# Attention and two feed-forward layers on one core: the transposes and the order of the kernel's opening

## The chip, the core and the metric

The kernel runs on one core of a Trainium2 chip. The core has five engines with queues of their own: TensorE (PE; its weight loads are PEld), VectorE (DVE), ScalarE (ACT), GpSimd (POOL) and SyncE (SP), which here issues every transfer. An engine takes its instructions in the order of the program and waits, on semaphores, for what the others owe it. The metric is the device time of one execution in microseconds (us); lower is better.

## The reference

An attention over chunks of 32 positions (16 to the left, 8 to the right, 8 memory positions, so 64 keys a chunk), 4 batches of 8 heads, 768 positions, 64 a head; its output, 3072 tokens of 512, goes through a layer with a squared ReLU and then through a gated layer.

```python
scores = scale * np.matmul(q_c, k_full.transpose(0, 1, 3, 2))
scores = scores - np.max(scores, axis=-1, keepdims=True)
a = np.exp(scores)
a = a / (np.sum(a, axis=-1, keepdims=True) + 1e-09)
out[:, :, c_start:c_end] = np.matmul(a, v_full)
...
h = x @ w_in            # 512 -> 2048
r = np.maximum(h, 0.0)
x = (r * r) @ w_out     # 2048 -> 512
...
g = x @ w_gate          # 512 -> 1536
silu = g * (1.0 / (1.0 + np.exp(-g)))
return (silu * (x @ w_val)) @ w_out
```

## The kernel before

Attention is cut into 32 units of 96 positions (three chunks) with all eight heads. The tokens are cut into eight blocks of four units (384 tokens). For each block the first layer runs over 16 slices f of 128 hidden columns: 12 hidden matmuls (`hidden_pe`: high weight by high x, high weight by low x, low weight by high x, four of each) into one of two PSUM banks `hbank`, then ReLU and square on ScalarE, the low part of the square on VectorE, and 12 projecting matmuls (`project_pe`) into the banks `yb`. Numbers are kept as a high and a low part of type fp32r. The gated layer comes after all blocks.

The weights of the first layer arrive as raw 64-bit words, 1 MB a slice, and are turned into the two parts during the first block: a scaling on ScalarE (`scale1`, L329), a shift and a joining on VectorE (`shift1`, L333; `join1`, L342), the high part on ScalarE (`hi1`, L346) and the low part on VectorE (`lo1`, L350). The first block therefore has on top of its matmuls the conversion of all 16 slices, the attention of its own four units (0 to 3), and that of the next block's (4 to 7).

The opening is written out by hand: `OPENING` is a list of 328 tokens, a letter for a step and a number for the unit u or the slice f, and the queue of each engine holds its steps in the order of the list. After the list a planner takes over. The letters, with the lines of the profile:

- Q, V: load of queries and keys, of values (SP, L132, L137). S: 24 score matmuls (PE, L153), for units 0 to 3 into `yb0`, later into `abank`.
- M maximum, D subtraction, A sum, I reciprocal, N scaling (DVE, L165 to L229); E exponential (ACT, L177); F, G: exponentials of later units (ACT, L211), K their scaling (DVE).
- T: transposes of units 0 to 3 on PE (L191), C: the copies of the result to `pT` (ACT, L197, L198); U, W: block transposes of later units on VectorE (L238), four and three instructions.
- O: eight value matmuls (PE, L257). X, Y: high and low part of the unit's tokens (ACT L268, DVE L272).
- L: load of a weight slice (SP, L321); p, s, j, h, l: its five conversion steps as above.
- a, b: the first eight and the last four hidden matmuls (PE, L359); r, q, t: ReLU and the two squares (ACT, L367 to L378); g: the low part (DVE, L384); c, d: projecting matmuls (PE, L403).

The transposes of units 0 to 3 write 32x32 pieces into two tiles: `yb1`, which c0 needs next, and `hbank[0]`, which a0 needs next.

```python
turned = [yb1[:, 0:2, 0:NH * 32].rearrange("p c (h q) -> p c h q", q=32)]
turned.append(hbank[0][:, 0:NH * 32].rearrange("p (h q) -> p h q", q=32))
```

Of the kernel before, what the change touches and what calls it, by code (L numbers as in the profile page):

```python
# [11 lines left out]
ALU = mybir.AluOpType  # L12
# [6 lines left out]
GQ = 96  # L19
# [16 lines left out]
NI = NH // 2  # L36
# [10 lines left out]
OPENING = """
Q0 Q1 Q2 S0 Q3 M0 V0 D0 L0 S1 E0 A0 M1 Q4 I0 D1 L1 N0 S2 E1 s0 p0 T0 M2 A1 C0 V1 D2 O0 L2 I1 E2 S3 N1 X0 s1
T1 p1 A2 V2 Y0 C1 M3 L3 O1 I2 N2 p2 D3 T2 X1 j0 V3 E3 L4 C2 A3 I3 h0 Y1 N3 O2 p3 L5 j1 T3 X2 l0 h1 C3 Y2 V4
s2 S4 p4 L6 j2 O3 X3 s3 h2 Y3 p5 l1 Q5 a0 l2 L7 b0 p6 a1 j3 r0 b1 M4 q0 L8 t0 a2 s4 h3 g0 b2 j4 r1 q1 c0 L9  # L50
t1 l3 r2 d0 h4 g1 a3 s5 F4 l4 V5 b3 L10 c1 j5 G4 d1 s6 a4 j6 L11 h5 K4 b4 r3 q2 l5 t2 c2 h6 L12 g2 U4 q3 d2
t3 a5 r4 q4 g3 L13 t4 b5 W4 p7 c3 l6 r5 d3 q5 L14 s7 p8 O4 j7 S5 p9 a6 g4 h7 s8 Q6 j8 b6 t5 V6 c4 X4 l7 L15
r6 q6 d4 t6 g5 a7 h8 M5 s9 p10 b7 l8 c5 F5 Y4 d5 j9 a8 G5 g6 s10 b8 j10 c6 h9 K5 r7 d6 h10 U5 r8 q7 W5 t7
p11 l9 O5 q8 t8 S6 g7 V7 p12 l10 a9 Q7 X5 M6 b9 p14 s11 c7 F6 g8 s12 d7 Y5 a10 j11 G6 b10 s13 c8 j12 h11 d8
K6 r9 h12 a11 l11 q9 t9 U6 b11 r10 c9 q10 t10 g9 p13 l12 d9 r11 W6 q11 t11 p15 j13 O6 S7 g10 h13 s14 a12 Q8
X6 M7 b12 l13 F7 c10 j14 d10 G7 g11 a13 s15 Y6 b13 j15 h14 c11 r12 K7 h15 d11 l14 a14 q12 t12 U7 r13 b14 q13
c12 t13 g12 W7 d12 r14 q14 t14 l15 O7 S8 g13 g14 a15 X7 M8 b15 Y7 F8 c13 d13 r15 q15 t15 g15
"""


# [1 line left out]
def attention_moe_moe_kernel(ctx, tc, att, w1, w2, out):  # L62
# [9 lines left out]
    pe, act, dve, pool, sp = nc.tensor, nc.scalar, nc.vector, nc.gpsimd, nc.sync  # L72
# [10 lines left out]
    hbank = [ps.tile([128, 512], F32, name=f"hbank{i}") for i in range(2)]  # L83
    abank, yb0, yb1 = (ps.tile([128, 2, 512], F32, name=n) for n in ("abank", "yb0", "yb1"))
# [15 lines left out]
    def convert(raw):  # L100
# [262 lines left out]

# [263 lines left out]
    for c in range(NC2):  # L627
        a = QB * (P2 + c // 4) + (12, 26, 40, 52)[c % 4]
# [170 lines left out]
```

## Time and profile before

| | us |
|---|---|
| median of three runs | 1187.6 (1186.94 to 1189.79) |
| the profiled execution | 1183.89 |
| its span, first to last instruction | 1182.1 |
| TensorE busy in the span | 1151.9 (97%) |
| VectorE busy | 680.3 (58%) |
| ScalarE busy | 600.9 (51%) |
| GpSimd busy | 354.7 (30%) |

The profile is one execution with a record of every instruction. A busy share is an average over stages with different limits: the page's table of forty slices shows TensorE at 4 tenths in the first slice (the first 30 us), 8 in the second and 9 in all others but the last. So the time without TensorE lies at the start, and the views below are all of the first 110 us, beside the list of TensorE's waits up to the end.

### The profile page before, as it was taken

To read this page: it belongs to the slowest core of one execution; us is meant where nothing else is said; L and a number is where in the kernel's file an instruction comes from. 1 tells how busy PE (TensorE), PEld (TensorE's weight loads), DVE (VectorE), ACT (ScalarE), POOL (GpSimd) and SP (SyncE) were. 2 spreads that over 40 slices of the span, in tenths; PEclk is the share of its full clock that TensorE was granted. 3 is DMA by queue.
4 is the path that set the end of the run, shared out by engine and by line. 5 is a ranking of instruction groups with operands and counts; after the bars stand their busy time and mean duration, and the time that the engine had idled before them with its cause. 6 is when DMAs were issued, how large, how long until landed. Compare 5 with 4: busy or idle time off the path is not lost.

```text
span 1182.1 us, 21404 instructions
## 1 busy us (share of the span) xinstructions
PE 1151.9 (97%) x8448; PEld 1096.0 (93%) x8448; DVE 680.3 (58%) x1220; ACT 600.9 (51%) x1466; POOL 354.7 (30%) x301
## 2 busy tenths in 40 slices
PE   4899999999999999999999999999999999999998
PEld 4889999999999999999999999999999999999996
DVE  6798444646446465452515576656766576655554
ACT  4787445556555464555553354444445444453442
POOL 0000000202002021000043465646556465654541
PEclk9999999999999999999999999999999999999999
DMA  8921204536255262530223323353234433343221
GB/s 307 379 86 51 75 29 154 185 105 244 78 161 192 77 213 108 177 105 1 72 81 112 129 91 101 127 190 103 90 129 146 153 105 105 104 143 129 94 99 54
DMA packets 49445, 150.29 MB, mean 127 GB/s; under 512 B 4800, under 2 KB 14528, under 8 KB 44992
## 3 DMA queue, kind: packets, MB, share of 16 engines
q1 hardware_dynamic: 49344, 148.92, 36.4%
q8 instruction: 66, 1.08, 0.4%
q14 instruction: 35, 0.29, 0.1%
HBM read 122.16 MB, written 26.74 MB: 126 GB/s over the span
## 4 chain that ended last, share of the span: by engine, by line
PE 94%; DVE 4%; issue 1%; ACT 1%; DMA 0%; SPq 0%; DVEq 0%; ACTq 0%
PE hbank L527 30%; PE yb L403 21%; PE hbank L359 21%; PE yb L597 11%; PE abank L597 6%; PE abank L257 2%; PE abank L153 2%; DVE pT L238 1%; DVE w L350 1%; DVE cut L342 1%; PE yb L191 0%; DVE wraw L333 0%; DMA qk<-in_att_dram 0%; PE yb L153 0%; DVE gl L384 0%
## 5 line engine op out<-in xcount | busy, mean ns | idle before, releaser
L92 POOL TENSOR_TENSOR w<-gvraw,w 128x512 fp32r<-128x512 f32 x192 | 247.6, 1311 | 295.1 <-ACT w L89 295.1
L359 PE MATMUL hbank<-x,w 128*128 128x384 f32 x1536 | 289.3, 336 | 0.6 <-ACT x L268 0.6
L527 PE MATMUL hbank<-w 128*128 128x384 f32 x1440 | 281.8, 335 | 0.1
L359 PEld LDWEIGHTS hbank<-x,w 128*128 128x128 f32 x1536 | 269.8, 189 | 1.2 <-ACT x L268 0.9
L527 PEld LDWEIGHTS hbank<-w 128*128 128x128 f32 x1440 | 254.5, 188 | 9.2 <-DVE tmp L567 0.4
L403 PE MATMUL yb<-gh,w 128*128 128x384 f32 x1024 | 205.0, 337 | 0.0
L384 DVE TENSOR_TENSOR gl<-r,gh 128x384 fp32r<-128x384 f32 x128 | 74.5, 582 | 186.4 <-ACT r L378 185.8
L403 PEld LDWEIGHTS yb<-gh,w 128*128 128x128 f32 x1024 | 178.7, 188 | 2.2
L446 POOL TENSOR_TENSOR wraw<-cut 128x256 f32<-128x256 f32 x24 | 20.2, 862 | 454.5 <-DVE mx L203 337.0
L536 ACT CAST uh<-tmp 128x384 fp32r<-128x384 f32 x96 | 49.4, 514 | 184.7 <-DVE tmp L571 152.3
L367 ACT ACTIVATE r<-hbank 128x384 f32<-128x384 f32 x128 | 62.8, 491 | 153.9 <-PE hbank L359 152.0
L597 PE MATMUL yb<-w,uh 128*128 128x512 f32 x384 | 119.6, 392 | 0.0
L527 PE MATMUL hbank<-z,w 128*128 128x384 f32 x576 | 115.7, 335 | 0.0
L403 PE MATMUL yb<-gl,w 128*128 128x384 f32 x512 | 113.2, 334 | 0.0
L527 PEld LDWEIGHTS hbank<-z,w 128*128 128x128 f32 x576 | 102.1, 188 | 4.2
L89 ACT CAST w<-gvraw 128x512 fp32r<-128x512 f32 x192 | 99.3, 564 | 3.1 <-POOL w L92 2.1
L403 PEld LDWEIGHTS yb<-gl,w 128*128 128x128 f32 x512 | 90.9, 188 | 0.0
L211 ACT ACTIVATE prob<-abank,mx 96x72 f32<-96x72 f32 x224 | 68.2, 315 | 42.7 <-DVE mx L203 39.5
L238 DVE STREAM_TRANSPOSE pT<-prob 32x256 f32<-32x256 f32 x196 | 85.2, 435 | 3.2
L597 PEld LDWEIGHTS yb<-w,uh 128*128 128x128 f32 x384 | 70.5, 188 | 9.5 <-ACT o L603 0.4
L597 PE MATMUL abank<-w,uh 128*128 128x512 f32 x192 | 74.9, 397 | 0.0
L378 ACT ACTIVATE r<-r 128x384 f32<-128x384 f32 x128 | 67.3, 526 | 3.8
(94 smaller groups left out, 1285.2 us busy)
## 6 DMA issues: line engine op xcount, KB each, us to landing
wraw<-in_w_dram SPq DMA_DIRECT2D x34, 1024.0 KB, 7.8
gvraw<-w2g SPq DMA_DIRECT2D x48, 512.0 KB, 3.5
gvraw<-w2g SPq DMA_DIRECT2D x48, 384.0 KB, 3.1
qk<-in_att_dram SPq DMA_DIRECT2D x28, 464.0 KB, 4.0
spare<-w2o SPq DMA_DIRECT2D x24, 512.0 KB, 4.4
v<-in_att_dram SPq DMA_DIRECT2D x32, 256.0 KB, 3.3
y1d<-ys SPq DMA_DIRECT2D x8, 768.0 KB, 3.9
w2g<-wraw SPq DMA_DIRECT2D x12, 512.0 KB, 2.9
```

Of the source, the lines that this page charges most:

```text
L89: act.copy(hi, src)
L92: lo_engine.tensor_tensor(lo, src, hi.bitcast(F32), ALU.subtract)
L211: act.activation(probs[u % 2][:, h, 0:WK], s["s"][:, r, i], AF.Exp, bias=s["mx"][:, r, i:i + 1], scale=SCALE, accum_out=s["sm"][:, h],)
L238: dve.transpose(pT[row:row + 32, :, 32 * c:32 * c + 32], probs[u % 2][32 * c:32 * c + 32, :, col:col + 32],)
L359: pe.matmul(hbank[f % 2][:, 0:n], wt[:, k * 128:(k + 1) * 128], x[:, k, 0:n], start=i == 0, stop=i == 3 * KD - 1,)
L367: act.activation(r, hbank[f % 2][:, 0:n], AF.Relu)
L378: act.activation(r, r, AF.Square)
L384: dve.tensor_tensor(gl, g["r"], g["gh"].bitcast(F32), ALU.subtract)
L403: pe.matmul(ybank[e][:, 0:nt_of[t]], wt[:, c:c + 128], gtile[t, f][g], start=f == 0 and p == 0, stop=f == NF1 - 1 and p == 2,)
L527: pe.matmul(to, wt[:, k * 128:k * 128 + 128], z[:, k], start=n == 0, stop=n == 5)
L536: act.copy(uh, u)
L597: pe.matmul(outs[j], u[:, c:c + 128], wt, start=f == 0 and p == 0, stop=f == NF2 - 1 and p == 2)
```

## The change

Four edits. First, a unit's transposes on TensorE (T) are done a head at a time, eight matmuls with a 96x96 identity in place of 56 with 32x32 pieces, all into `yb1`. Second, five copies on ScalarE (C) bring the pieces of that result to where `pT` wants them, in place of two. Third, slice 0's hidden product may be done in two parts: x0, y0 and w0 are its three groups of four matmuls on the 288 columns of units 0 to 2, and v0 is all twelve on the 96 columns of unit 3. Fourth, the list `OPENING` is laid out anew. Two memsets of the old targets go, and a step that the list did not use.

```diff
@@ -43,18 +43,19 @@
+TURNED = (((0, 64, 0),), ((0, 32, 32), (32, 64, 64)), ((0, 64, 64), (64, 72, 32)))
 OPENING = """
-Q0 Q1 Q2 S0 Q3 M0 V0 D0 L0 S1 E0 A0 M1 Q4 I0 D1 L1 N0 S2 E1 s0 p0 T0 M2 A1 C0 V1 D2 O0 L2 I1 E2 S3 N1 X0 s1
...
+Q0 Q1 Q2 S0 V0 Q3 M0 D0 V1 S1 E0 L0 A0 M1 D1 L1 I0 S2 E1 N0 A1 T0 I1 p0 N1 Q4 M2 C0 D2 L4 s0 S3 j0 E2 T1 p1
...
@@ -180,22 +181,17 @@
-    turned = [yb1[:, 0:2, 0:NH * 32].rearrange("p c (h q) -> p c h q", q=32)]
-    turned.append(hbank[0][:, 0:NH * 32].rearrange("p (h q) -> p h q", q=32))
+    turned = yb1[0:WK, :, 0:NI * GQ].rearrange("p b (h q) -> p b h q", q=GQ)
 
     def at_turn_0(u):
         for h in range(NH):
-            for c in range(3):
-                for col, row in PIECES[c]:
-                    to = turned[0][:, c] if c < 2 else turned[1]
-                    pe.matmul(
-                        to[row:row + 32, h], probs[u % 2][32 * c:32 * c + 32, h, col:col + 32],
-                        eye[32 * c:32 * c + 32], start=True, stop=True, tile_position=(32 * c, row),
-                    )
+            pe.transpose(turned[:, h // NI, h % NI], probs[u % 2][:, h, 0:WK], eye)
 
     def at_turned_0(u):
-        act.copy(pT[:, :, 0:64].rearrange("p h (c q) -> p c h q", c=2), turned[0])
-        act.copy(pT[:, :, 64:96], turned[1])
+        for c in range(3):
+            q = slice(32 * c, 32 * c + 32)
+            for a, b, row in TURNED[c]:
+                act.copy(pT[row:row + b - a, :, q].rearrange("p (b h) q -> p b h q", b=2), turned[a:b, :, :, q])
@@ -349,15 +341,15 @@
-    def hidden_pe(t, f, part):
-        n = nt_of[t]
+    def hidden_pe(t, f, part, cols=None):
+        cols = cols or slice(0, nt_of[t])
...
             pe.matmul(
-                hbank[f % 2][:, 0:n], wt[:, k * 128:(k + 1) * 128], x[:, k, 0:n],
+                hbank[f % 2][:, cols], wt[:, k * 128:(k + 1) * 128], x[:, k, cols],
                 start=i == 0, stop=i == 3 * KD - 1,
             )
@@ -647,22 +639,23 @@
-    for o in turned:
-        dve.memset(o, 0.0)
-    eye = ap.tile([GQ, 32], F32, name="eye")
+    eye = ap.tile([GQ, GQ], F32, name="eye")
     pool.memset(eye, 1.0)
-    for c in range(3):
-        pool.affine_select(
-            out=eye[32 * c:32 * c + 32], in_=eye[32 * c:32 * c + 32], pattern=[[-1, 32]], base=0,
-            channel_multiplier=1, compare_op=ALU.is_equal, fill=0.0,
-        )
+    pool.affine_select(
+        out=eye, in_=eye, pattern=[[-1, GQ]], base=0, channel_multiplier=1, compare_op=ALU.is_equal, fill=0.0,
+    )
...
+        "x": lambda f: hidden_pe(0, f, range(KD), slice(0, 3 * GQ)),
+        "y": lambda f: hidden_pe(0, f, range(KD, 2 * KD), slice(0, 3 * GQ)),
+        "w": lambda f: hidden_pe(0, f, range(2 * KD, 3 * KD), slice(0, 3 * GQ)),
+        "v": lambda f: hidden_pe(0, f, range(3 * KD), slice(3 * GQ, 4 * GQ)),
```

TensorE, from the end of T3 to the first hidden matmuls. Before: the last two groups of T3's 32x32 matmuls, S4, O3, and then a0.

```order
L191 MATMUL yb1_79<-eye_96,prob1_84 32x32 x4
L191 MATMUL hbank0_75<-eye_96,prob1_84 32x32 x3
L153 MATMUL abank_77<-early_104 32x64 x24
L257 MATMUL abank_77<-pT_85,v_458 64x96 x8
L359 MATMUL hbank0_75<-x0_275,w_469 128x384 x4
L359 MATMUL hbank0_75<-x1_276,w_469 128x384 x4
```

The same place now: T2, O1, T3, O2, x0, S4, O3, y0, w0 and the first rows of v0.

```order
L188 MATMUL yb1_79<-eye_94,prob0_83 72x96 x8
L253 MATMUL abank_77<-pT_85,v_139 64x96 x8
L188 MATMUL yb1_79<-eye_94,prob1_84 72x96 x8
L253 MATMUL abank_77<-pT_85,v_295 64x96 x8
L351 MATMUL hbank0_75<-x0_269,w_281 128x288 x4
L154 MATMUL abank_77<-early_100 32x64 x24
L253 MATMUL abank_77<-pT_85,v_324 64x96 x8
L351 MATMUL hbank0_75<-x1_270,w_281 128x288 x4
L351 MATMUL hbank0_75<-x0_269,w_281 128x288 x4
L351 MATMUL hbank0_75<-x0_269,w_281 128x96 x4
```

A unit's transposes are one row of eight, and the first hidden matmuls stand ahead of S4 and O3.

VectorE, from the third unit's Y (an L272 row) to past the fourth's. Before: Y2, s2, j2, s3, Y3, l1, l2, j3 (the numbers behind wraw, cut and w tell the slices apart).

```order
L272 TENSOR_TENSOR x1_276<-abank_77,x0_275 128x4x96
L333 TENSOR_SCALAR wraw_285<-wraw_285 128x1024
L342 SCALAR_TENSOR_TENSOR cut_579<-wraw_285 128x1024
L333 TENSOR_SCALAR wraw_383<-wraw_383 128x1024
L272 TENSOR_TENSOR x1_276<-abank_77,x0_275 128x4x96
L350 TENSOR_TENSOR w_544<-cut_484,w_544 128x1024
L350 TENSOR_TENSOR w_591<-cut_579,w_591 128x1024
L342 SCALAR_TENSOR_TENSOR cut_622<-wraw_383 128x1024
```

Now: j3, Y2, l2, s4, j4, l3, Y3 and the maximum of unit 4.

```order
L334 SCALAR_TENSOR_TENSOR cut_369<-wraw_307 128x1024
L268 TENSOR_TENSOR x1_270<-abank_77,x0_269 128x4x96
L342 TENSOR_TENSOR w_365<-cut_348,w_365 128x1024
L329 TENSOR_SCALAR wraw_228<-wraw_228 128x1024
L334 SCALAR_TENSOR_TENSOR cut_424<-wraw_228 128x1024
L342 TENSOR_TENSOR w_410<-cut_369,w_410 128x1024
L268 TENSOR_TENSOR x1_270<-abank_77,x0_269 128x4x96
L198 TENSOR_REDUCE mx_442<-abank_77 96x8
```

Six conversion steps (s4, j3, j4, l1, l2, l3), which stood behind Y3, stand ahead of it.

ScalarE, around the copies of unit 2. Before: E3 (the exponential), the two copies, h0, p3.

```order
L177 ACTIVATE prob1_84<-prob1_84 96x8x72
L197 COPY pT_85<-yb1_79 128x2x8x32
L198 COPY pT_85<-hbank0_75 128x8x32
L346 CAST w_469<-cut_456 128x1024
L329 ACTIVATE wraw_383<-wraw_383 128x1024
```

Now: E3, p4, p2, the five copies, X1, h1, p3.

```order
L178 ACTIVATE prob1_84<-prob1_84 96x8x72
L325 ACTIVATE wraw_228<-wraw_228 128x1024
L325 ACTIVATE wraw_279<-wraw_279 128x1024
L194 COPY pT_85<-yb1_79 64x8x32
L194 COPY pT_85<-yb1_79 32x8x32 x2
L194 COPY pT_85<-yb1_79 64x8x32
L194 COPY pT_85<-yb1_79 8x8x32
L264 CAST x0_269<-abank_77 128x4x96
L338 CAST w_350<-cut_321 128x1024
L325 ACTIVATE wraw_307<-wraw_307 128x1024
```

Two scalings that need loaded weights (p4, p2) stand ahead of unit 2's copies. Behind the list, the rows of all engines are the same in both kernels.

## Rows read from the trace of the kernel before

**Rows 1.** The page, part 1: busy us, share of the span, instructions.

```profile
PE 1151.9 (97%) x8448; PEld 1096.0 (93%) x8448; DVE 680.3 (58%) x1220; ACT 600.9 (51%) x1466; POOL 354.7 (30%) x301
```

**Rows 2.** TensorE's waits from 38 us on: us in total, times, longest.

```profile
PE abank L257 <- ACT gh L373: 2.9, 1, 2.9
PE abank L257 <- DVE pT L238: 1.8, 2, 1.5
```

**Rows 3.** TensorE's timeline: start us, duration us, line, tile, count, [idle before, releaser].

```profile
7.37 1.09 PE L153 MATMUL yb<-early 64*32 64x64 f32 x48 [1.99 <-DVE prob L173]
...
14.16 0.21 PE L191 MATMUL yb<-eye,prob 32*32 32x32 f32 x1 [1.57 <-issue]
...
15.70 1.55 PE L257 MATMUL abank<-pT,v 128*64 128x96 f32 x16 [0.99 <-ACT pT L198]
...
20.37 0.28 PE L191 MATMUL yb<-eye,prob 32*32 32x32 f32 x5 [1.71 <-issue]
...
35.24 0.43 PE L153 MATMUL abank<-early 64*32 64x64 f32 x5 [3.92 <-issue]
...
37.73 8.54 PE L359 MATMUL hbank<-x,w 128*128 128x384 f32 x36 [0.58 <-ACT x L268]
...
108.09 0.88 PE L257 MATMUL abank<-pT,v 128*64 128x96 f32 x16 [0.30 <-DVE pT L238]
```

**Rows 4.** TensorE by stretch: stretch, us, busy (matmul rows), clock, DMA share, GB/s.

```profile
0.00:13.50 13.50, 4.26 (x221) 1.00 0.84 319
13.50:19.50 6.00, 3.50 (x127) 1.00 0.91 346
...
29.00:34.00 5.00, 2.12 (x128) 1.00 1.02 416
```

**Rows 5.** The instruction queue, 0 to 40 and 32.75 to 33.0 us: packets, MB, share.

```profile
q8 instruction: 6, 0.10, 0.9%
...
q8 instruction: 1, 0.02, 24.7%
```

**Rows 6.** VectorE's timeline, with the columns of rows 3.

```profile
5.51 0.17 DVE L159 MEMSET yb<- 32x128 f32 x1 [2.55 <-PE yb L153]
...
27.31 1.22 DVE L342 SCALAR_TENSOR_TENSOR cut<-wraw 128x1024 int32<-128x1024 int32 x1
28.44 1.22 DVE L350 TENSOR_TENSOR w<-cut,w 128x1024 fp32r<-128x1024 f32 x1
...
30.05 0.68 DVE L333 TENSOR_SCALAR wraw<-wraw 128x1024 int32<-128x1024 int32 x1
...
37.71 0.56 DVE L272 TENSOR_TENSOR x<-abank,x 128x384 fp32r<-128x384 f32 x1 [5.12 <-ACT x L268]
...
74.62 3.14 DVE L238 STREAM_TRANSPOSE pT<-prob 32x256 f32<-32x256 f32 x7
```

**Rows 7.** VectorE by stretch, with the columns of rows 4.

```profile
8.06:38.24 30.18, 20.27 (x38) 1.00 0.90 353
38.24:108.05 69.81, 66.12 (x105) 1.00 0.40 156
```

**Rows 8.** The transposing matmuls (L191) alone, with the columns of rows 4.

```profile
0.00:40.00 40.00, 6.29 (x448) 1.00 0.87 335
```

**Rows 9.** ScalarE's timeline around C0, with the columns of rows 3.

```profile
14.79 0.59 ACT L197 COPY pT<-yb 128x512 f32<-128x512 f32 x1 [1.05 <-PE hbank L191]
15.27 0.38 ACT L198 COPY pT<-hbank 128x256 f32<-128x256 f32 x1
15.54 0.69 ACT L177 ACTIVATE prob<-prob 96x576 f32<-96x576 f32 x1
```

**Rows 10.** Weight loads issued at 5.94 (L2) and 17.66 us (L3): count, KB, us to landing.

```profile
wraw<-in_w_dram SPq DMA_DIRECT2D x1, 1024.0 KB, 14.1
...
wraw<-in_w_dram SPq DMA_DIRECT2D x1, 1024.0 KB, 5.7
```

**Rows 11.** TensorE by stretch at the first hidden matmuls, with the columns of rows 4.

```profile
38.00:42.00 4.00, 4.00 (x13) 1.00 1.01 422
42.00:46.00 4.00, 4.00 (x24) 1.00 1.02 420
```

More of the change, by code (lines that the diff above doesn't have):

```diff
@@ L45 @@
 WC = 1024
+TURNED = (((0, 64, 0),), ((0, 32, 32), (32, 64, 64)), ((0, 64, 64), (64, 72, 32)))
 EARLY = (1, 2, 3, 4)
 OPENING = """
-Q0 Q1 Q2 S0 Q3 M0 V0 D0 L0 S1 E0 A0 M1 Q4 I0 D1 L1 N0 S2 E1 s0 p0 T0 M2 A1 C0 V1 D2 O0 L2 I1 E2 S3 N1 X0 s1
[L49 to L57, printed above, removed]
+Q0 Q1 Q2 S0 V0 Q3 M0 D0 V1 S1 E0 L0 A0 M1 D1 L1 I0 S2 E1 N0 A1 T0 I1 p0 N1 Q4 M2 C0 D2 L4 s0 S3 j0 E2 T1 p1
+M3 O0 L2 h0 D3 A2 C1 I2 N2 V2 l0 X0 T2 L3 E3 Y0 p4 s1 O1 j1 p2 V3 A3 C2 L5 I3 N3 s2 X1 T3 j2 h1 L6 p3 Y1 s3
+O2 h2 l1 X2 j3 C3 V4 x0 Q5 Y2 l2 S4 h3 L7 O3 s4 p5 j4 y0 X3 w0 p6 l3 L8 h4 Y3 M4 v0 p7 l4 L9 a1 r0 s5 q0 j5
+b1 t0 a2 F4 g0 V5 s6 b2 L10 j6 c0 h5 s7 r1 d0 l5 q1 a3 r2 L11 q2 j7 t1 b3 t2 g1 c1 G4 g2 s8 L12 d1 s9 a4 r3
+K4 h6 b4 U4 q3 L13 c2 t3 r4 q4 g3 d2 t4 W4 a5 p8 L14 l6 p10 b5 c3 j8 r5 q5 g4 t5 d3 L15 s10 h8 O4 g5 h7 s11
+S5 a6 l8 p9 Q6 M5 b6 X4 p11 c4 V6 l7 F5 j9 d4 a7 j10 G5 b7 Y4 c5 s14 s12 r6 d5 K5 q6 a8 h9 U5 r7 b8 t6 c6 q7
+W5 h10 g6 t7 l9 p12 d6 O5 j11 r8 q8 S6 V7 t8 g7 a9 Q7 h11 M6 X5 b9 l10 F6 c7 g8 j12 d7 G6 a10 l11 b10 Y5 h12
+s13 c8 K6 r9 d8 q9 U6 r10 a11 t9 p13 b11 g9 W6 c9 p14 r11 j13 d9 q11 O6 q10 l12 h13 S7 j14 a12 t10 Q8 t11 X6
+M7 b12 h14 g10 c10 g11 F7 l14 d10 a13 l13 G7 s15 b13 Y6 c11 r12 K7 r13 d11 q13 U7 q12 a14 t12 p15 b14 g12 W7
+c12 t13 r14 q14 j15 d12 t14 O7 g13 h15 g14 S8 l15 a15 X7 M8 b15 c13 Y7 r15 q15 t15 d13 F8 g15
 """
@@ L333, in shift1 @@
         dve.tensor_scalar(lower, lower, 29, None, ALU.logical_shift_right)
-    def shift1_pool(f):
-        lower = words1(f)[0]
-        pool.tensor_scalar(lower, lower, 29, None, ALU.logical_shift_right)
     def join1(f):
@@ L662, in attention_moe_moe_kernel @@
         "Q": at_load, "V": at_load_v, "S": at_scores, "D": at_sub_0, "E": at_exp_0, "A": at_sum_0, "I": at_invert,
-        "N": at_scale, "T": at_turn_0, "C": at_turned_0, "O": at_pv, "X": at_x_hi, "Y": at_x_lo, "F": at_exp_1,
+        "N": at_scale, "T": at_turn_0, "C": at_turned_0,
+ "O": at_pv, "X": at_x_hi, "Y": at_x_lo, "F": at_exp_1,
         "G": at_exp_2, "K": at_norm, "U": at_turn_1, "W": at_turn_2, "L": load1, "p": scale1, "s": shift1,
-        "z": shift1_pool, "j": join1, "h": hi1, "l": lo1,
+        "j": join1, "h": hi1, "l": lo1,
+        "x": lambda f: hidden_pe(0, f, range(KD), slice(0, 3 * GQ)),
+        "y": lambda f: hidden_pe(0, f, range(KD, 2 * KD), slice(0, 3 * GQ)),
+        "w": lambda f: hidden_pe(0, f, range(2 * KD, 3 * KD), slice(0, 3 * GQ)),
+        "v": lambda f: hidden_pe(0, f, range(3 * KD), slice(3 * GQ, 4 * GQ)),
         "M": lambda u: (at_max_0 if u < BLOCKS[0] else at_max)(u),
```

## The prediction

> **What bounds the kernel now.** I read the page's first part first. TensorE is busy for 1151.9 of 1182.1 us [rows 1], so only some 30 us can be had, and the next question is where they lie. The list of TensorE's waits from 38 us on answers it: 2.9 + 1.8 us in front of the value products (L257), which end with the one at 108.09 us, and nothing else of note [rows 2, 3]. So after that TensorE sets the time alone, and whatever this change does happens before it. There are two stretches.
>
> From the start to the first hidden matmul at 37.73 us TensorE mostly waits. Three of its waits carry the label "issue", that is, no engine and no load was late: 1.57, 1.71 and 3.92 us [rows 3]. What they have in common is a count: 221 matmul rows start before the first, 127 between the first and the second, and 128 from 29 us to the third [rows 4]. A queue of its own, marked instruction, moves six packets of together 0.10 MB in the first 40 us, and one of them passes at 32.75 to 33.0 us, 2.2 us before the last of the three waits ends at 35.24 [rows 5]. I read this as the engine's program arriving in blocks: 128 rows with their weight loads are 256 instructions, and 0.10 MB / 6 is about 16 KB. A block ended at about 8.46 us (221 rows had started by the first wait, and 221 - 128 = 93 is the end of S1), and the next one was there at 14.16; the one after it at 20.37: 5.7 and 6.2 us each [rows 3, 4]. The longest of the three stood inside S4 and held S4, O3, X3 and Y3 in a row: VectorE sat 5.12 us until Y3 could run [rows 6].
>
> From 37.73 to 108.09 us VectorE sets the pace. It is busy for 66.1 of 69.8 us there [rows 7], and it releases O5, O6 and O7 late. (For O5 the list of waits names ScalarE; but VectorE's seven block transposes for it end at 77.76 us, right when TensorE goes on [rows 6].) So an earlier first matmul is worth nothing by itself; VectorE's stream has to get ahead too. In the 30.2 us before, VectorE is busy for only 20.3 [rows 7]: that is the reserve.
>
> **The change part by part.** *Transposes.* 448 matmul rows of L191, busy for 6.3 us [rows 8], that is 112 rows and 1.6 us a unit, become 8 matmuls a unit. One 96-column product of L257, the nearest in size, shows two rows, so I count 16 rows a unit; one to four rows each are possible, 8 to 32. The time: 16 such rows took 1.55 us there [rows 3]. I take 1.5 us, with ends at 0.8 and 3.1. So the array's own time hardly changes; the count does. The rows before Y3 are now 5 x 48 (S) + 4 x 16 (T) + 4 x 16 (O) + 12. The block ends, at rows 93, 221 and 349, come to lie at the end of S1 (8.5 us), the last matmul of T1 (17.5) and inside S4 (32): 9 and 14 us apart, where a block needs 6.2. I put all three waits at zero.
>
> The Trainium skill speaks against that: "Runtime: NRT & Kernel Launch", section "Instruction fetch mechanics", has the same blocks of 16 KiB and 256 instructions, but says that crossing one is mostly hidden, since dispatch is slower than refill. The rows above do not agree, by up to 3.92 us. By that rule the waits would have another cause and could stay: the first rival.
>
> *Copies.* ScalarE's two copies a unit become five. Before, the pair holds it from 14.79 to 15.54 us, 0.75 us, and the copy of 256 elements a partition, the size of all five, 0.27 of that [rows 9]. Five take 5 x 0.27 + 0.1 = 1.45 us: 0.7 us more a unit, 2.8 in all, on an engine that is 51% busy [rows 1]. C0 and C1 delay T1 and O1, C3 delays O3; each is in the chain below.
>
> *Memsets, identity.* Two memsets leave VectorE before 3 us, where it waits for the first scores until 5.51 anyway [rows 6]; one select takes the place of three on GpSimd, 9 us ahead of need. Zero.
>
> *Split of the first hidden product.* 12 matmuls become 12 of 288 columns and 12 of 96. They run before and during the wait for unit 3, and take away 12 from what follows it. hbank is no longer a target of the transposes, so x0 need not wait for C3.
>
> *Order, the head.* VectorE's instructions from A0 (8.06 us) to Y3 are those of before plus s4, j3, j4, l1, l2, l3. An s takes 0.68 us, a j 1.13 from start to start, and an l, of the same size and duration, as much [rows 6]: 0.7 + 5 x 1.13 = 6.3 us. Without a single wait Y3 ends at 8.06 + 20.3 + 6.3 = 34.7 us. Walking the queues by these durations I find waits worth 1.0 us (D3 for T1, and results read by the next instruction), and 0.6 us because V1 (256 KB) now stands ahead of the first weight: 36.3 us, 2.0 earlier than before (38.27 [rows 6]) although VectorE has done 6.3 us more. The chain beside it: S3 at 14.9 (after D2), T1 16.0 to 17.5, O0 to 19.1, C1 to 20.6, T2 and O1 to 23.7, C2 (behind p2, which waits for its load until about 22.5) to 25.2, T3 to 27.3, O2 28.0 to 29.6, X2 30.1, x0 to 31.2, S4 to 32.3, O3 to 33.9, X3 34.5; Y1, Y2, Y3 each find their operand there 0.8 to 1.6 us before VectorE comes to them. After Y3, eight 96-column matmuls and the queue ahead of them end at 37.8 us. If transposes take 3.1 us, D3 and T3 slip and this becomes 39.3; without any wait it is 36.2.
>
> *Order, the loads.* SyncE's queue now has V1 ahead of L0, and L4 ahead of L2; V2 waits for O0 with L3 behind it, V3 for O1 with L5 and L6, V4 for O2 with L7 to L9. L2 landed 14.1 us after its issue at 5.94, at 20.0 [rows 10]; 1 MB more ahead of it is 2.5 us at the 420 GB/s of this stretch [rows 11], so 22.5. L3 is issued at about 19.5 and has L2, V2 and itself to wait for: 25.7; p3 wants it at 26.6. In the chain above both have room, 0.5 and 0.9 us.
>
> *From there to O7, TensorE.* Before, 36 hidden matmuls took 8.54 us [rows 3], 13 in the first 4.0 us and 24 in the next 4.0 [rows 11]: 0.31 and 0.167 us for 384 columns, so the lower level (1.2 GHz) and then the upper (2.4 GHz), while the granted-clock column reads 1.00 in both. Before it rose, TensorE had worked without long breaks since 35.24. In the new order such work begins at 30.2, so I take the upper level from 37.8 on: 24 matmuls (f = 1 and 2) at 0.173 are 4.2 us, and c0 starts at 42.0 instead of 46.27. From c0 to O7 it took 108.09 - 46.27 = 61.8 us with 4.7 us of waits [rows 2]; without them 57.1, so O7 at 99.1.
>
> *From there to O7, VectorE.* Its 66.1 busy us lose s4, j3, j4, l1 to l3, and j15, which now stands behind W7: 7.5 us. W7 ends at 36.3 + 58.6 = 94.9 us, or 98.6 with all the 3.7 us of idle time that it had. Both are before 99.1, so TensorE has become the bound. *Behind W7* j15, h15 and l15 are still to come, with O7 and S8 (1.6 us) as cover; I charge 0.3 us.
>
> **Sum.** O7 comes 108.09 - 99.1 = 9.0 us earlier, less 0.3: 8.7 us. The rest of the program keeps its order on every engine. The profiled execution took 1183.89 us, 1.8 us more than its span, and lies 3.7 us under the median of the three runs, 1187.6. I take 8.7 us off the median: 1178.9 us.
>
> **The rivals.** *The issue waits stay (0.14).* If the 3.92 us belong to S4 and not to the count of instructions, S4 ends at 36.2, and Y3 and the first full product come 3.7 us later: gain 5.0, 1182.6 us. For: the page's rule. Against: the even count. The same size comes if the clock stays low for the first 24 matmuls: 24 x 0.14 = 3.3 us.
>
> *VectorE stays the bound (0.22).* If the head ends at 38 us (slow transposes, L0 late) and the waits of before all return, W7 ends at 38 + 58.6 + 3.7 = 100.3, and with 0.5 to 1.5 us for ScalarE's longer queue at 101: gain 7 us, 1180.6 us.
>
> *ScalarE's queue behind a load, mild and severe.* p2 stands ahead of C2 and p3 ahead of X2 and C3, and L3 is issued only after O0. Mild (0.11): L3 lands 14.1 us after its issue at 19.5, the longest in the rows; 33.6 instead of 26.6, so all of the gain but 1.7 us is gone: 1185.9. Severe (0.05): one block wait of 3.92 us holds O0 besides; L3 lands at 37.5, 10.9 us late: 1189.8, slower than before. It decides once L3 lands later than 26.6 + 8.7 = 35.3 us. Against both: 14.1 us was seen with five loads out at once [rows 10], 5.7 for the load issued after the first V that waited.
>
> **How the numbers follow.** The forecast has 0.48: 1178.9, by the head's ends (36.2 to 39.3) 1177.3 to 1180.4, and with the runs' own spread (1186.94 to 1189.79) 1175.5 to 1182. The range of 8 in 10 takes in VectorE and issue waits, and leaves the mild and severe load cases out: 1175.5 to 1184. This kernel's measurement can tell 0.3%, 3.6 us, from no change. Faster by more: 0.48 + 0.22 + 0.14 = 0.84. Within: the mild case and 0.02 of the severe, 0.13. Slower: 0.03, the severe case with its waits a little longer than worked out.
>
> **What would show it.** Right: no "issue" wait over 0.5 us on TensorE before 40 us; Y3 ending near 36; c0 near 42; no wait of TensorE over 0.5 us in front of O5, O6, O7, and O7 near 99. Wrong: an issue wait inside S4 again; p2 or p3 waiting for its load with C2 or X2 behind it; T over 2.5 us; or VectorE over 95% busy and O6 waiting for W6, as before.

## The result and the profile after

| | before | after |
|---|---|---|
| median of four runs each, us | 1187.92 (1186.94 to 1189.79) | 1177.12 (1175.71 to 1177.77) |
| ratio, 95% interval | | 0.9906 [0.9888, 0.9923] |
| profiled execution, us | 1183.89 | 1175.71 |
| its span, us | 1182.1 | 1174.0 |

The changed kernel is 10.8 us faster; 1178.9 was forecast, with a range of 1175.5 to 1184. The two profiled executions lie 8.2 us apart, so the steps below are held against 8.2, and the other 2.6 us are a question of their own (the experiments on the kernel before bear on it).

The page of the profile after, part 1 (busy us, share of the span, instructions):

```profile
PE 1151.1 (98%) x8044; PEld 1094.3 (93%) x8044; DVE 679.4 (58%) x1218; ACT 605.5 (52%) x1478; POOL 354.3 (30%) x299
```

Against [rows 1], TensorE has 404 rows less (448 - 32 for the transposes, + 12 for the split) and works 0.8 us less. So some 7 of the 8 us were idle time. TensorE's timeline after shows where (start us, duration us, line, tile, count, [idle before, releaser]; L188 is T, L154 S, L253 O, L351 the hidden product, L395 the projecting one):

```profile
11.61 1.47 PE L188 MATMUL yb<-eye,prob 96*72 96x96 f32 x8
15.00 1.10 PE L154 MATMUL yb<-early 64*32 64x64 f32 x48 [1.92 <-DVE prob L174]
16.02 1.49 PE L188 MATMUL yb<-eye,prob 96*72 96x96 f32 x8
17.45 1.27 PE L253 MATMUL abank<-pT,v 128*64 128x96 f32 x16
20.79 0.85 PE L188 MATMUL yb<-eye,prob 96*72 96x96 f32 x8 [2.08 <-ACT pT L194]
22.00 1.55 PE L253 MATMUL abank<-pT,v 128*64 128x96 f32 x16 [0.36 <-DVE x L268]
25.84 1.48 PE L188 MATMUL yb<-eye,prob 96*72 96x96 f32 x8 [2.29 <-ACT pT L194]
28.15 1.55 PE L253 MATMUL abank<-pT,v 128*64 128x96 f32 x16 [0.84 <-DVE x L268]
30.28 1.33 PE L351 MATMUL hbank<-x,w 128*128 128x288 f32 x4 [0.58 <-ACT x L264]
31.68 1.10 PE L154 MATMUL abank<-early 64*32 64x64 f32 x48
32.71 1.55 PE L253 MATMUL abank<-pT,v 128*64 128x96 f32 x16
34.19 5.36 PE L351 MATMUL hbank<-x,w 128*128 128x288 f32 x32
39.76 2.35 PE L351 MATMUL hbank<-x,w 128*128 128x384 f32 x12 [0.21 <-ACT r L359]
41.94 1.55 PE L395 MATMUL yb<-gh,w 128*128 128x384 f32 x8
...
99.85 0.88 PE L253 MATMUL abank<-pT,v 128*64 128x96 f32 x16
```

No wait is put down to "issue" any more; S4 (31.68) stands whole, where before it was cut by 3.92 us [rows 3]. A unit's transposes are one row of eight. And O7, the last row, comes at 99.85 in place of 108.09 [rows 3], 8.24 us earlier, with nothing in front of it. All of TensorE's waits from 38 us to the end of the program (us in total, times, longest):

```profile
PE yb L589 <- DVE ul L532: 0.6, 1, 0.6
PE yb L395 <- DVE gl L376: 0.4, 1, 0.4
PE hbank L351 <- ACT r L359: 0.2, 1, 0.2
```

The 2.9 and 1.8 us of [rows 2] are gone. VectorE by stretch, from A0 to Y3 and from there to 98.35 us, just before the end of W7 (stretch, us, busy and instructions, clock, DMA share, GB/s):

```profile
8.06:36.24 28.18, 27.14 (x44) 0.76 0.96 375
36.24:98.35 62.11, 58.62 (x97) 1.00 0.45 174
```

The reserve of [rows 7] is used: 20.27 of 30.18 us busy then, 27.14 of 28.18 now. The instruction queue in the first 40 us moves half of what it did [rows 5]:

```profile
q8 instruction: 3, 0.05, 0.5%
```

### The profile page after: what moved, and what is told of

Same layout as the page of the kernel before. It is cut to its first block, busy times and chain, and to the rows that moved or that the text cites. A ratio compares the mean times of both kernels' runs of the same rounds, so it can differ in the third digit from the quotient of the medians.

```text
span 1174.0 us, 20605 instructions
## 1 busy us (share of the span) xinstructions
PE 1151.1 (98%) x8044; PEld 1094.3 (93%) x8044; DVE 679.4 (58%) x1218; ACT 605.5 (52%) x1478; POOL 354.3 (30%) x299
## 4 chain that ended last, share of the span: by engine, by line
PE 93%; DVE 4%; DMA 1%; ACT 1%; issue 0%; SPq 0%; DVEq 0%; ACTq 0%
PE hbank L519 30%; PE yb L395 22%; PE hbank L351 21%; PE yb L589 11%; PE abank L589 6%; PE abank L253 2%; PE abank L154 1%; DMA wraw<-in_w_dram 1%; DVE wraw L329 1%; DVE pT L234 0%; DVE cut L334 0%; DVE w L342 0%; DVE prob L225 0%; DVE gl L376 0%; DMA qk<-in_att_dram 0%
## 5 line engine op out<-in xcount | busy, mean ns | idle before, releaser
L351 PE MATMUL hbank<-x,w 128*128 128x384 f32 (+1 forms) x1548 | 289.8, 335 | 0.8 <-ACT x L264 0.6
L351 PEld LDWEIGHTS hbank<-x,w 128*128 128x128 f32 x1548 | 269.6, 189 | 2.1 <-ACT x L264 0.9
L395 PE MATMUL yb<-gh,w 128*128 128x384 f32 x1024 | 205.0, 337 | 0.0
L395 PEld LDWEIGHTS yb<-gh,w 128*128 128x128 f32 x1024 | 178.7, 188 | 2.2
L395 PE MATMUL yb<-gl,w 128*128 128x384 f32 x512 | 113.3, 334 | 0.4 <-DVE gl L376 0.4
L395 PEld LDWEIGHTS yb<-gl,w 128*128 128x128 f32 x512 | 90.9, 188 | 0.7 <-DVE gl L376 0.7
L365 ACT ACTIVATE gh<-r 128x384 fp32r<-128x384 f32 x128 | 67.3, 528 | 3.5
```

The costliest lines, as they stand in the source:

```text
L351: pe.matmul(hbank[f % 2][:, cols], wt[:, k * 128:(k + 1) * 128], x[:, k, cols], start=i == 0, stop=i == 3 * KD - 1,)
L365: act.activation(gh, gtile[t, f]["r"], AF.Square)
L395: pe.matmul(ybank[e][:, 0:nt_of[t]], wt[:, c:c + 128], gtile[t, f][g], start=f == 0 and p == 0, stop=f == NF1 - 1 and p == 2,)
```

## The experiments

Theory A, that of the prediction: TensorE's unlabelled waits come when 128 matmul rows have been used up faster than the next block of instructions arrives, so the short transposes take them away; but VectorE paces what follows, so this alone gains only a part, and the new order, which puts six conversion steps into VectorE's idle time, is needed for the rest. There are three rivals: the waits belong to places (S4 beside the loads) and not to the count; the transposes alone do it; or the order alone does it. The texts in quotes, each written before its run, use the letters B and C for the rivals of that run only.

**Transposes alone.** The kernel before with the new transposes, copies and identity, and its old order of the opening.

```diff
-            for c in range(3):
-                for col, row in PIECES[c]:
...
+            pe.transpose(turned[:, h // NI, h % NI], probs[u % 2][:, h, 0:WK], eye)
```

> The kernel before with the changed transposes and copies alone; the order of the opening stays, slice 0 is not split. Theory A (the issue waits come from the count of instructions, and VectorE's lead decides the rest): no issue wait over 0.5 us on TensorE before 40 us; S4 and O3 are no longer held, Y3 ends at 33 to 35 us instead of 38.27, VectorE gets 4 to 5 us ahead, O5 to O7 are still released by VectorE with 4 to 5 us of waits; time 1182 to 1184.5 us, ratio 0.996. Rival B (the waits belong to the places, not to the count): an issue wait of 3 to 4 us in S4 again, 1187 us or more. Rival C (the count explains all of the gain): no waits in front of O5 to O7 either, 1178 us.

Measured: 1181.0 (1179.24 to 1182.5) against 1185.9 (1181.26 to 1189.33), ratio 0.9968 [0.995, 0.9987]: 4.9 us faster, and 1.0 us under the 1182 to 1184.5 us expected. Its timelines of TensorE and then VectorE (L399 is c0, L253 are O5 to O7, L268 on DVE is Y3):

```profile
29.66 1.10 PE L154 MATMUL abank<-early 64*32 64x64 f32 x48 [0.26 <-DVE x L268]
...
42.53 1.55 PE L399 MATMUL yb<-gh,w 128*128 128x384 f32 x8
...
74.29 0.88 PE L253 MATMUL abank<-pT,v 128*64 128x96 f32 x16 [2.86 <-ACT gh L369]
...
89.98 0.88 PE L253 MATMUL abank<-pT,v 128*64 128x96 f32 x16 [1.43 <-DVE pT L234]
...
104.52 0.88 PE L253 MATMUL abank<-pT,v 128*64 128x96 f32 x16 [0.29 <-DVE pT L234]
```

```profile
33.94 0.56 DVE L268 TENSOR_TENSOR x<-abank,x 128x384 fp32r<-128x384 f32 x1 [1.87 <-ACT x L264]
```

No issue wait is left: S4 is whole at 29.66 and Y3 ends at 34.5, 1.7 us before that of the changed kernel. Yet O7 comes 4.7 us after the changed kernel's, because the waits in front of O5, O6 and O7 stand as they did before. That is the half of theory A on VectorE: an early first product is worth nothing where VectorE cannot follow. So the transposes alone are not the whole gain.

**Order alone.** The changed kernel with the old transposes, two copies and three selects; the third target lies in the other bank, since x0 now begins early.

```diff
-    turned = yb1[0:WK, :, 0:NI * GQ].rearrange("p b (h q) -> p b h q", q=GQ)
+    turned = [yb1[:, 0:2, 0:NH * 32].rearrange("p c (h q) -> p c h q", q=32)]
+    turned.append(hbank[1][:, 0:NH * 32].rearrange("p (h q) -> p h q", q=32))
```

> The changed kernel with the old 56 transposing matmuls and two copies a unit (the third target in the other hidden bank, so that x0 need not wait for it). Theory A: issue waits return at matmul rows 221, 349, 477, 605 and 733, that is in T0, T1, T2, T3 and S4, 5 to 9 us in all; D2, D3 and S4 are held, Y3 ends at 39 to 41 us instead of 36.2, O7 comes at 102 to 106 us; time 1181 to 1184.5 us. Rival B (the order alone does it, VectorE's queue hides what TensorE loses): Y3 below 37 us, 1177 to 1178.5 us.

Measured: 1180.86 (1179.79 to 1184.86), ratio 0.9967 [0.9949, 0.9986]: 5.0 us faster, and 0.1 us under the 1181 to 1184.5 us expected. TensorE's two issue waits, and what VectorE pays for the second (its subtraction for unit 3 reads scores that stand behind that wait):

```profile
14.26 0.21 PE L192 MATMUL yb<-eye,prob 32*32 32x32 f32 x1 [1.46 <-issue]
...
20.37 0.27 PE L192 MATMUL yb<-eye,prob 32*32 32x32 f32 x3 [3.20 <-issue]
```

```profile
20.78 1.01 DVE L174 TENSOR_TENSOR prob<-yb,mx 96x288 f32<-96x288 f32 x2 [2.83 <-PE hbank L192]
...
39.00 0.55 DVE L273 TENSOR_TENSOR x<-abank,x 128x384 fp32r<-128x384 f32 x1
```

I had expected five such waits of together 5 to 9 us; there are two, of 4.7. The rows at which the other three were due (the middle of T2, of T3, and S4) come after TensorE had waited 1.0 us and more for ScalarE or VectorE, and no wait for instructions shows there. The 2.83 us go straight into Y3, which ends at 39.6 instead of 36.2, and O7 comes at 102.88, 5.2 us before that of the kernel before. (Behind O7 this run took 1.9 us longer than the kernel before: 1.4 of them are one wait in the gated layer, L524 for VectorE, which the first profiles of before and after do not have.) The changed kernel's medians, 1177.1 to 1177.3 us in its three groups of runs, lie 8.6 to 8.8 us under the 1185.9 beside which both halves ran; the halves gain 4.9 and 5.0. So neither gives the whole, and the rival that the order alone does it falls too.

**The count or the place.** The kernel before, with 32 idle matmuls of 32x32 ahead of S0 (they write into a bank that is not yet used).

```diff
+    for _ in range(32):
+        pe.matmul(hbank[1][0:32, 0:32], eye[0:32], eye[0:32], start=True, stop=True, tile_position=(0, 0))
```

> The kernel before with 32 small matmuls (64 rows) put first on TensorE, where it waits for the first load until 4.3 us; nothing else is changed, their result is not used. Theory A (the program arrives in blocks of 128 matmul rows): the issue waits keep their row count from the program's start (221, 349, 605, 733), so they stand elsewhere: 13 rows into T0, 13 rows into S3, in T1, T2 and T3; none in S4. The one in T0 is shorter by 1 us or more because its block is asked for earlier. Time 1183 to 1188 us. Rival B (the waits belong to the places): waits of 1.5, 1.7 and 3.9 us at the same instructions as before, in T0 77 rows in, in T1 and in S4 43 rows in, 1187 to 1188 us.

Measured: 1185.73 (1182.44 to 1188.29), ratio 1.0008 [0.999, 1.0026]. TensorE's timeline (L153 is S, L191 T):

```profile
2.36 3.62 PE L662 MATMUL hbank<-eye 32*32 32x32 f32 x64 [2.36 <-POOL eye L655]
5.90 1.09 PE L153 MATMUL yb<-qk 64*32 64x64 f32 x48
...
17.04 0.53 PE L153 MATMUL yb<-early 64*32 64x64 f32 x13
19.21 0.88 PE L153 MATMUL yb<-early 64*32 64x64 f32 x35 [1.65 <-issue]
...
24.31 0.27 PE L191 MATMUL hbank<-eye,prob 32*32 32x32 f32 x3 [3.08 <-issue]
...
33.69 0.27 PE L191 MATMUL hbank<-eye,prob 32*32 32x32 f32 x3 [0.92 <-issue]
```

The 32 matmuls are 64 rows. The cut moves into S3, 13 rows after its begin: 64 + 3 x 48 + 112 + 16 + 13 = 349 = 221 + 128 rows from the start. The next wait comes after another 128 rows, in T1 (477 rows begin before 24.3 us), a third, of 0.92 us, in T3, and S4, which stood 3.92 us before [rows 3], is whole. That the waits belong to places falls: they go with the count of rows. Not every block end is a wait: the two due 13 rows into T0 and in T2 do not show, though waits were expected there. (The time is the same as before. The three waits sum to 5.7 us, those of the first profile of before to 7.7, and S0 starts 1.6 us later.)

**The kernel before, again.** Two more profiles of the unchanged kernel, for the spread of its runs, which goes from 1181.3 to 1189.3 us.

> The kernel before, unchanged, for a second profile. Its runs so far lie between 1181.3 and 1189.3 us, those of the changed kernel between 1175.7 and 1177.8. Theory: the spread is that of the issue waits, which last as long as the block of the program takes behind the data loads. Then a profile with another time shows the same three waits at rows 221, 349 and 733 with other lengths, and Y3 and O7 are shifted by as much as the time: a run of 1187 us has about 3 us more of them than the 7.2 us of the first profile. Rival: the spread comes later in the program; then the waits and O7 (108.1) are the same within 0.5 us whatever the time.

> The same once more: O7's start against the time of the run should lie on the same line, 1 us for 1 us.

Measured: 1186.53 and 1184.09 us. In the first, all five block ends from row 221 to Y3 are waits (two of them below; S4's is 3.92 again), and O7 comes at 110.73; in the second only three, the one in S4 lasts 2.36 us, and O7 comes at 108.28:

```profile
24.95 0.28 PE L191 MATMUL yb<-eye,prob 32*32 32x32 f32 x4 [0.94 <-issue]
...
31.32 0.21 PE L191 MATMUL hbank<-eye,prob 32*32 32x32 f32 x1 [2.37 <-issue]
```

```profile
33.46 0.43 PE L153 MATMUL abank<-early 64*32 64x64 f32 x5 [2.36 <-issue]
```

Time less O7 is 1075.8 us in all three profiles of before (1183.89 - 108.09, 1186.53 - 110.73, 1184.09 - 108.28) and in that of after (1175.71 - 99.85 = 1075.9). So what differs between these three runs of the kernel before happens ahead of O7. Between the first profile and the run of 1186.53 it is the issue waits: 7.7 us in all in the one (the first profile has a fourth, of 0.46 us, at 29.21), 10.0 in the other, and O7 2.6 us later. In the run of 1184.09 they are only 5.5, yet O7 is no earlier. There Y3 ends 1.8 us earlier than in the first profile, but the first 36 hidden matmuls take 9.32 us in place of 8.54, so that c0 is only 1.0 us ahead, and behind O5, at a lower granted clock, that is lost too (the last section shows it). So the waits are not the only thing that varies. For the 2.6 us of the result this is a likely cause, not a shown one: no run at the median of that group, 1187.9, was profiled. In three groups of runs the changed kernel had medians of 1177.1 to 1177.3, and the kernel before beside it 1187.9, 1183.5 and 1186.2: gains of 10.8, 6.2 and 8.8 us. The 10.8 of the result is the largest of the three.

**Without the split.** The changed kernel, with slice 0's hidden product whole (a0 and b0 after Y3) in place of x0, y0, w0 and v0.

```diff
-O2 h2 l1 X2 j3 C3 V4 x0 Q5 Y2 l2 S4 h3 L7 O3 s4 p5 j4 y0 X3 w0 p6 l3 L8 h4 Y3 M4 v0 p7 l4 L9 a1 r0 s5 q0 j5
+O2 h2 l1 X2 j3 C3 V4 Q5 Y2 l2 S4 h3 L7 O3 s4 p5 j4 X3 p6 l3 L8 h4 Y3 M4 a0 b0 p7 l4 L9 a1 r0 s5 q0 j5
```

> The changed kernel with a0 and b0, twelve matmuls of 384 columns, where v0 stands, in place of x0, y0, w0 and v0. Theory A (TensorE is the bound from Y3 on): a0 starts with Y3's end at 36.2, S4 and O3 come 1.3 us earlier; twelve full matmuls come in place of twelve of 96 columns, so c0 moves from 41.9 to 42.5 to 45, depending on the clock's level, and O7 by the same; time 1178 to 1180.5 us. Rival B (VectorE is the bound in front of O5 to O7): O7 within 0.5 us of 99.85, 1177 us.

Measured: 1177.52 (1176.62 to 1179.57), ratio 0.9946 [0.9928, 0.9964]. Its c0 starts at 44.18 in place of 41.94 and O7 comes at 101.42, 1.6 us later than in the first profile of after; but its first weight landed 1.3 us later too, and its Y3 ends 0.64 us later. So the split is worth about 1 us in the trace, an estimate, and too little to be seen in the medians (1177.52 against 1177.1 to 1177.3). Neither expectation holds whole: c0 lies in theory A's range, the median under it. The split is no large part of the gain.

**Y earlier.** In the profile of after, VectorE does Y1 at 27.55 although its operand had been there since 26.3, and O2 waits for it. This kernel moves Y1 ahead of j2 and Y3 ahead of l3; a run of the changed kernel stands beside it.

```diff
-M3 O0 L2 h0 D3 A2 C1 I2 N2 V2 l0 X0 T2 L3 E3 Y0 p4 s1 O1 j1 p2 V3 A3 C2 L5 I3 N3 s2 X1 T3 j2 h1 L6 p3 Y1 s3
-O2 h2 l1 X2 j3 C3 V4 x0 Q5 Y2 l2 S4 h3 L7 O3 s4 p5 j4 y0 X3 w0 p6 l3 L8 h4 Y3 M4 v0 p7 l4 L9 a1 r0 s5 q0 j5
+M3 O0 L2 h0 D3 A2 C1 I2 N2 V2 l0 X0 T2 L3 E3 Y0 p4 s1 O1 j1 p2 V3 A3 C2 L5 I3 N3 s2 X1 T3 h1 L6 p3 Y1 j2 s3
+O2 h2 l1 X2 j3 C3 V4 x0 Q5 Y2 l2 S4 h3 L7 O3 s4 p5 j4 y0 X3 w0 p6 Y3 l3 L8 h4 M4 v0 p7 l4 L9 a1 r0 s5 q0 j5
```

> The changed kernel with two steps of VectorE exchanged: Y1 ahead of j2 and Y3 ahead of l3. In its trace O2 waits for Y1 until 28.15 us although its operand X1 is there at 26.3, and the chain from O2 through X2, x0, S4 and O3 to y0, w0 and v0 has no other wait. If that chain sets TensorE's start, O2 comes 0.8 us earlier, c0 at about 41.2 instead of 41.9 and O7 0.5 to 0.8 us earlier; the median 1176 to 1177 us. If VectorE's total is what counts, nothing changes, since its sum of work is the same.

> The changed kernel again, beside the other kernels of this call: 1176 to 1178 us, no issue wait before 40 us, and a spread of its runs under 3 us, against some 8 us for the kernel before. If its spread is as wide as that of the kernel before, the issue waits are not what makes the spread.

Measured: 1178.11 (1176.13 to 1179.1), beside 1177.29 (1175.41 to 1177.82) for the changed kernel: nothing won. O2 no longer waits for VectorE, but what it wins is lost again ahead of y0: x0 waits 0.86 us for X2 in place of 0.58, and S4, which had no wait, stands 0.60 us for Y2, which is where it was on VectorE, behind j3. Beside the third profile of the changed kernel, whose first weight landed as late (13.69 us, here 13.62), O2 comes 0.8 us earlier and y0 at 34.94 in place of 34.98. The rest is a wait that the changed kernel has as well. TensorE's S4, ScalarE's timeline and TensorE's a2 in this kernel:

```profile
32.44 1.09 PE L154 MATMUL abank<-early 64*32 64x64 f32 x48 [0.60 <-DVE x L268]
```

```profile
40.02 1.18 ACT L325 ACTIVATE wraw<-wraw 128x1024 f32<-128x1024 f32 x1 [2.48 <-DMA wraw<-in_w_dram]
41.08 0.50 ACT L359 ACTIVATE r<-hbank 128x384 f32<-128x384 f32 x1
```

```profile
41.63 2.36 PE L351 MATMUL hbank<-x,w 128*128 128x384 f32 x12 [1.35 <-ACT r L359]
```

ScalarE stands 2.48 us at p7, for the eighth weight, with r0 in the queue behind it, and a2 waits for r0, since the two use the same bank. The same is there in the changed kernel, from 1.35 us at p7 (0.21 at a2) in its first profile to 2.92 (1.62 at a2) in the third, below.

**r0 ahead of p7.** If ScalarE's queue holds a2, p7 moved behind r0, q0 and t0 takes the wait at a2 away. One kernel does this alone, one together with the earlier Y, and the changed kernel runs beside them.

```diff
-O2 h2 l1 X2 j3 C3 V4 x0 Q5 Y2 l2 S4 h3 L7 O3 s4 p5 j4 y0 X3 w0 p6 l3 L8 h4 Y3 M4 v0 p7 l4 L9 a1 r0 s5 q0 j5
-b1 t0 a2 F4 g0 V5 s6 b2 L10 j6 c0 h5 s7 r1 d0 l5 q1 a3 r2 L11 q2 j7 t1 b3 t2 g1 c1 G4 g2 s8 L12 d1 s9 a4 r3
+O2 h2 l1 X2 j3 C3 V4 x0 Q5 Y2 l2 S4 h3 L7 O3 s4 p5 j4 y0 X3 w0 p6 l3 L8 h4 Y3 M4 v0 l4 L9 a1 r0 s5 q0 j5
+b1 t0 a2 F4 p7 g0 V5 s6 b2 L10 j6 c0 h5 s7 r1 d0 l5 q1 a3 r2 L11 q2 j7 t1 b3 t2 g1 c1 G4 g2 s8 L12 d1 s9 a4 r3
```

> The changed kernel with p7, which needs the eighth weight load, behind r0, q0, t0 and F4 on ScalarE instead of ahead of them. In the traces p7 waits 1.3 to 2.5 us for its load at 37 to 40 us and r0, which lets a2 use its bank, stands behind it. If that queue holds TensorE, a2 has no wait for r0, g0 comes 1 to 1.5 us earlier, c0 0.2 us earlier where the load came early and up to 1.3 us where it came late: median 1176 to 1177 us, the changed kernel's highest runs gone. If j7, which now comes later, holds VectorE, nothing is won.

> The exchange of Y1 and j2, Y3 and l3 together with p7 behind r0. Alone, the first brought O2 forward and lost it again at a2, which waited 1.35 us for r0 behind p7. If that is so, both together give c0 at 41.2 to 41.5 and O7 0.5 to 0.8 us ahead of the changed kernel: 1175.5 to 1176.5 us. Otherwise the same as the run with p7 alone.

> The changed kernel once more, beside the two variants of this call: 1176 to 1178 us.

Measured: r0 first 1175.51 (1175.39 to 1177.42), both 1176.67 (1175.76 to 1179.21), the changed kernel 1177.34 (1175.63 to 1180.19); against before 1186.18, ratios of 0.9913 [0.99, 0.9926], 0.9923 [0.9909, 0.9937] and 0.9926 [0.9911, 0.994]. ScalarE of the changed kernel in this group, and its a2:

```profile
13.69 1.15 ACT L325 ACTIVATE wraw<-wraw 128x1024 f32<-128x1024 f32 x1 [2.62 <-DMA wraw<-in_w_dram]
40.51 1.12 ACT L325 ACTIVATE wraw<-wraw 128x1024 f32<-128x1024 f32 x1 [2.92 <-DMA wraw<-in_w_dram]
```

```profile
42.05 2.37 PE L351 MATMUL hbank<-x,w 128*128 128x384 f32 x12 [1.62 <-ACT r L359]
```

And with r0 first, ScalarE and TensorE, where the hidden products run through without a wait although the first weight landed even later (14.15):

```profile
14.15 1.15 ACT L325 ACTIVATE wraw<-wraw 128x1024 f32<-128x1024 f32 x1 [3.15 <-DMA wraw<-in_w_dram]
38.69 0.49 ACT L359 ACTIVATE r<-hbank 128x384 f32<-128x384 f32 x1 [0.64 <-PE hbank L351]
```

```profile
35.46 7.42 PE L351 MATMUL hbank<-x,w 128*128 128x288 f32 x44
42.72 1.55 PE L395 MATMUL yb<-gh,w 128*128 128x384 f32 x8
```

c0 comes at 42.72 in place of 44.27 and O7 at 100.27 in place of 102.14. With both changes the wait at a2 is gone too, but c0 comes at 41.97 and O7 at 99.49, where the first profile of the changed kernel has 41.94 and 99.85. The c0 expected, 41.2 to 41.5, was missed: S4 waits 0.60 us for Y2 here as well, so the earlier Y brings nothing to c0. That the wait at a2 goes is shown; whether the kernel is faster is not, since the intervals overlap and 1.8 us between medians of five and six runs is less than they spread. It is the lowest median of all, and the version I would go on with.

## Why the prediction was right

*What bounds it: right in both parts.* The blocks of 128 rows are shown by the shifted kernel, whose waits moved with the count. (There were four waits for instructions in the first profile and not three: the fourth, 0.46 us at 29.21, stands in T3 where the count asks for it.) VectorE as the pace of what follows is shown by the transposes alone, which made Y3 3.8 us earlier than [rows 6] and left every wait in front of O5 to O7.

*Transposes.* Forecast 1.5 us and 16 rows a unit; measured 1.47 to 1.49 (0.85 for T2) and 8 rows, one per matmul. The block ends so lie later still than I placed them, within O0 and at the first rows of v0 (221 = 208 + 13 and 349 = 348 + 1, where O0 begins behind row 208 and v0 behind row 348), and none is a wait.

The Trainium skill's rule ("Runtime: NRT & Kernel Launch", section "Instruction fetch mechanics"), that crossing such a block is mostly hidden, agrees with the trace of the changed kernel and not with that of the one before, by up to 3.92 us. What decides here is how many rows a stretch uses in the time that a block takes to arrive: 4.9 to 6.4 us from the end of one wait to the end of the next in the run of before that has five of them. In the first profile the block that T2 needs was there 4.1 us after the wait in T1 had ended (20.37 to 24.48), too soon for a wait that is listed.

*Copies: mis-sized.* Five take 1.9 us, not 1.45. ScalarE's timeline after:

```profile
13.26 1.91 ACT L194 COPY pT<-yb 64x256 f32<-64x256 f32 x5
```

I had counted each at the 0.27 us from the start of such a copy to the start of the exponential behind it [rows 9]; five in a row follow each other at 0.38 us from start to start, which is the full duration of the copy in the same row, although the smallest holds only 8 partitions of 128. T3 waited 2.29 us for C2, but O2 was held by Y1 anyway, until 28.15: in this run the miss cost nothing on the path.

*The head.* The chain came out within 0.5 us at each step shown: S3 14.9 and 15.00, T3's end 27.3 and 27.3, O2 28.0 and 28.15, x0's end 31.2 and 31.6, O3's end 33.9 and 34.3. Y3 ended at 36.23, forecast 36.3, by luck, since two errors cancel: VectorE was busy for 27.1 us instead of 26.6, and waited for 1.0 instead of 1.6. The 0.6 us for a late first weight were not paid in this run (12.2 us) but in others (12.7 to 14.2).

*To c0.* Forecast 42.0, measured 41.94. The clock did as taken: TensorE's granted clock, by stretch (columns of [rows 4]), is 0.50 from 25 to 30 us, the lower level (1.2 GHz), and 1.00 from 36 us on, the upper (2.4 GHz), after it had worked without long breaks since 30.28:

```profile
20.00:25.00 5.00, 2.40 (x24) 0.67 0.80 275
25.00:30.00 5.00, 3.03 (x24) 0.50 1.01 401
36.00:42.00 6.00, 5.79 (x38) 1.00 1.00 402
```

*From c0 to O7.* Forecast 57.1 us without waits, measured 57.9. One wait of 0.43 us for g6 is in it. The forecast was also 0.3 us too low, because I had counted from the end of the hidden products, 46.27, while c0's row in the kernel before starts earlier, and had taken 4.7 us of waits off where the rows add up to 4.61:

```profile
46.10 1.55 PE L403 MATMUL yb<-gh,w 128*128 128x384 f32 x8
```

108.09 - 46.10 - 4.61 is 57.4, and 0.1 us is left open. This is the term that makes the gain of the profile smaller: O7 came 8.24 us earlier, not 9.0. Behind W7 I had charged 0.3 us, and the time from O7 to the end grew by 0.06 (1075.8 to 1075.86): 8.2 us in all against 8.7. VectorE's 58.6 busy us are 58.62 up to 98.35 us, and W7 ends at 98.57, at the late end of the 94.9 to 98.6 forecast and 1.3 us before O7: the rival "VectorE stays the bound" did not come about, by 1.3 us.

*The total.* I took 8.7 off the median. The mechanism and the size in the trace were right to 0.5 us. That the median fell by 10.8 is the part I left out: the runs of the kernel before vary, in part by their issue waits. The run of 1186.53 us has 2.4 us more of them than the first profile, and against its O7 the changed kernel's comes 10.9 us earlier. That the runs of the result's group were like it is not shown, and with the other groups' gains of 6.2 and 8.8 us, how near the median came to 1178.9 is partly luck. The rival of ScalarE behind a load was real, but at another place: not p2 or p3, as I wrote, but p7 ahead of r0, for 0.2 to 1.6 us.

## What to carry to other kernels

Where an engine waits and nothing is late, count its instructions from one such wait to the next: an even count is a sign that the program itself is what it waits for, some idle instructions put ahead of the stretch can test it, and fewer, larger instructions in that stretch take the wait away. An earlier start is worth only what the next engine can follow, so look in the same stretch for that engine's idle time and move its later work there; here either half alone gave 5 us and both 6 to 11, by the group of runs. And before a step that waits for a load is put into an in-order queue, look who stands behind it.

## What the runs showed of the hardware

Waits for instructions are not a fixed cost: the same kernel had four of them in its first profile, five and three in the two others, 7.7, 10.0 and 5.5 us in all, and the one in S4 lasted 3.92, 3.92 and 2.36 us. Runs of the kernel before spread over 8.5 us, and those of the changed one, which has no such wait, over 2.1 to 4.6 (under 3 had been expected). So the waits are a part of the spread and not all of it. Other times vary too: the landing of the first weight varied from 12.2 to 14.2 us, p7's wait for the eighth in the changed kernel from 1.35 to 2.92, and the time from O7 to the end from 1075.7 to 1077.7 in the profiles of all kernels here.

The granted clock fell in one run of the kernel before, in the middle of the work: after the wait of 2.87 us in front of O5, O5 took 1.55 us, where it took 0.88 in the other two. Its timeline, and TensorE by stretch:

```profile
76.88 1.55 PE L257 MATMUL abank<-pT,v 128*64 128x96 f32 x16 [2.87 <-ACT gh L373]
```

```profile
74.00:80.00 6.00, 3.13 (x67) 0.68 0.08 15
```

It cost that run 1.2 us: up to O5 it was 1.0 us ahead of the first profile (76.88 against 77.87), and O7 came 0.2 us behind it. O5, S6 and the hidden product behind them took 2.7 us longer; 1.4 of that came out of O6's wait for VectorE, which the other two have and this run has not. In the changed kernel's first profile the clock rose early, after TensorE had worked without a break from 15.00 to 18.7: T2 took 0.85 us, where T1 and T3 took 1.49 and 1.48. By O1, after waits of 2.08 and 0.36 us, it was down again (1.55 us). This moved nothing, since O2 waited for VectorE's Y1.
